# Block attention feeding a gated long convolution on one core: contiguous key loads for the first twelve heads, another order of the first head's work, and copies moved between engines

## The chip, the cores and the metric

The kernel runs on one core of one Trainium2 chip. The metric is device time in microseconds of one launch, lower is better. A core has five engines with an instruction queue each, which run in the order in which the kernel issues: TensorE (PE, with its weight loads shown as PEld), VectorE (DVE), ScalarE (ACT), GpSimd (POOL) and SyncE (SP), which here only issues DMAs. Instructions wait for one another through semaphores.

## The reference, cut to what matters

Inputs `q`, `k`, `v` have the shape (4, 8, 768, 64): 4 batches of 8 heads, so 32 heads of 768 positions, 64 wide.

```
k_rep = k.reshape(B, H, 12, 64, D).mean(axis=3)            # one mean key per block of 64
gate_scores = einsum('bhsd,bhnd->bhsn', q, k_rep)          # later blocks are ruled out
top_idx = argsort(gate_scores)[..., -3:]                   # 3 blocks for each query, and its own
scores = q @ k^T / 8, masked to those blocks and causally
attn = softmax(scores);  x = attn @ v                      # x: (4, 768, 512), heads side by side

proj = x @ w_proj;  x1, x2, x3 = its three parts of 512
x2_conv = irfft(rfft(x2) * rfft(filter_fft))               # along the 768 positions
out = (x1 * x2_conv * x3) @ w_out
```

## The kernel before

**Slots.** The program is a loop over slots, three for each head (`n`, `s`), written out by hand: `scores` of the slot, then `normalise` and the outputs' transposes of earlier heads, stores, `diagonals`, the preparation of coming heads (`prepare`, or `prepare_first` for heads 0 and 1), the set-up pieces entered by `at(n, s, ...)`, the convolution units of the batch before, and last `product` of the slot before. No scheduler moves anything: each engine's order is the order of these calls. Ahead of the loop stands a start written out call by call.

**One head.** A head's queries and keys lie in one fp16 tile, `qk16s[n % 3]` (128 partitions x [2, 6, 128]): t = 0 holds the query, and beside it the query's rounding rest (`query_rest` on VectorE, `low_query` on POOL); t = 1 holds the key (`cast_key`, on POOL) and 12 columns that mark its block (`key_mask`, on POOL, from `eblk`, written once for each of the three tiles). The tile has to be turned, so that the 64 + 12 columns become partitions, into `turned[n]` (`qkT`). For heads 0 to 11 (`PE_HEADS = 12`) TensorE does it (`turn_pe`, six transposes each for t = 0 and 1, into a PSUM bank of `ps_one`), and VectorE or ScalarE copies the result out. From head 12 on SP issues a DMA transpose (`turn_query`).

**The gate.** Key sums of a block (`krp`, fp32 products of keys with `eblk`) are formed on TensorE for heads 0 to 11 (`key_sums_mm`, `key_sums_copy`, `key_sums_turn`, `key_sums_split`, which leaves `kr`), and from head 12 on come from accumulating DMAs on POOL's queue (`add_blocks`, `k_blk`) and sums on VectorE. `gate` multiplies queries by them and finds the third highest on VectorE, with `cbias` ruling out later blocks and `ownm` keeping the own one; the result `gm16` is 0 or -1. `turn_mask` transposes it on TensorE, for two heads at a time from head 2 on, and copies it into rows 64 to 75 of the query part of `qkT`. There it meets the 12 block columns of the keys, so that `scores` gets the mask with the same product.

**Scores and products.** `scores` makes 2 to 4 products in a PSUM tile `sps`, ScalarE takes the exponential (`ex`, 1024, 896 or 768 wide by slot), POOL clears what lies above the diagonal, and `product` multiplies by the values.

**Loads.** Each head's `q`, `k` and `v` come by SP in 192 KB, with position `128 c + p` in chunk c of partition p:

```
k_r = k.rearrange("b h (c p) d -> b h p c d", p=P)
nc.sync.dma_start(keys[g][:, i], k_r[divmod(n, H)])
```

A partition thus gets six rows of 256 bytes from six places. `eblk`[p, c, n] says whether position `128 c + p` is in block n. Weights come by POOL's queue, cast to fp16 (`weights`); `wo` is first read by the output unit (`op`) of batch 0, at head 17.

**Warm products.** `warm(times)` issues 128x512 products on zeros into a PSUM tile that nobody reads (`unread`). At the start five stand ahead of the first key sums, two behind head 0's turns, two ahead of head 0's mask.

**The convolution** of a batch runs in 24 slots behind its eight heads: `x2` (X2), its transform (F1, products `f1a`, `f1b` with VectorE's `t` and POOL's `PQ`), `x13a` and `x13b` (X13, `x1sb` on ScalarE, `gx` on VectorE), the inverse (F2, `f2a`, `f2b`, `yes`, `yy`, `yT`) and the output (O, `op`, `osb`). The sines of the transform are made in the start (`phase_mm`, `phase_round`, `phase_turns`, `sines`). All of them share the four `ps_one` banks with the masks' transposes and the turns.

Of the kernel before, what the change touches and what calls it, by code (L numbers as in the profile page):

```python
# [12 lines left out]
ALU = mybir.AluOpType  # L13
# [4 lines left out]
def kernel(  # L18
# [70 lines left out]

    q_r = q.rearrange("b h (c p) d -> b h p c d", p=P)  # L90
    k_r = k.rearrange("b h (c p) d -> b h p c d", p=P)
    v_r = v.rearrange("b h (c p) d -> b h p c d", p=P)
    NH = B * H

# [18 lines left out]
    def load_key(n):  # L113
        g, i = group_of[n]
        if i == 0:
            keys[g] = kpool.tile([P, KG, SC, D], FP32, name="k_nat", tag="k_nat")
        nc.sync.dma_start(keys[g][:, i], k_r[divmod(n, H)])

    def load_query(n):
        queries[n] = hpool.tile([P, SC, D], FP32, name="q_nat", tag="q_nat")  # L120
# [6 lines left out]
    for n in range(3):  # L127
# [16 lines left out]


    eblk = const.tile([P, SC, NBLK], FP32)
    nc.gpsimd.memset(eblk, 0.0)
    nc.gpsimd.affine_select(
        out=eblk[0:64], in_=eblk[0:64], compare_op=ALU.not_equal,
        fill=1.0, base=0, pattern=[[-2, SC], [1, NBLK]], channel_multiplier=0)  # L150
    nc.gpsimd.affine_select(
        out=eblk[64:128], in_=eblk[64:128], compare_op=ALU.not_equal,
        fill=1.0, base=-1, pattern=[[-2, SC], [1, NBLK]], channel_multiplier=0)

# [11 lines left out]
    def key_mask(i):  # L168
        nc.gpsimd.tensor_scalar(qk16s[i][:, 1, :, D:D + NBLK], in0=eblk, scalar1=MASK, scalar2=0.0,
                                op0=ALU.mult, op1=ALU.add)  # L170

    id_f32 = const.tile([H * NBLK, H * NBLK], FP32)
    nc.gpsimd.memset(id_f32, 0.0)
# [10 lines left out]
    def small_constants(half):  # L184
        rows_ = slice(64 * half, 64 * half + 64)
        if half == 0:
            nc.gpsimd.memset(cbias, 0.0)
        nc.gpsimd.affine_select(
            out=cbias[rows_], in_=cbias[rows_], compare_op=ALU.is_ge,
            fill=-CBIG, base=half, pattern=[[2, SC], [0, 2], [-1, NBLK]], channel_multiplier=0)  # L190
        if half == 1:
            for h in range(2):
                nc.gpsimd.tensor_scalar(ownm[:, :, h, :], in0=eblk, scalar1=1.0, scalar2=-1.0,
                                        op0=ALU.mult, op1=ALU.add)

    FC = const.tile([P, HC, F], fp)
    FS = const.tile([P, HC, F], fp)
# [190 lines left out]
                                    qk16s[n % NB].rearrange("p t c s -> p (t c s)"))  # L388


    def turn_pe(n, t, copy):

        if n not in turned:
            turned[n] = augp.tile([P, 2, SC, P], fp, name="qkT", tag="qkT")
        rows_ = D + NBLK if t else P
        tp = ps_one.tile([P, S], fp, name="tp", tag="one", padded_shape=[P, 2 * 512])
        for c in range(SC):
            nc.tensor.transpose(tp[0:rows_, P * c:P * (c + 1)], qk16s[n % NB][:, t, c, 0:rows_],
                                id_f16)
        copy(turned[n][0:rows_, t], tp[0:rows_, :].rearrange("n (c s) -> n c s", c=SC))  # L400

    def cast_value(n):
        vals[n] = v16s[n % NB]
# [330 lines left out]
    for i in range(2):  # L734
        half = slice(2 * i, 2 * i + 2)
        at(3 + i, 1, weights, wp, moe_w_proj, slice(Dm, 2 * Dm), half)
        at(5 + i, 0, weights, wp, moe_w_proj, slice(2 * P * i, 2 * P * (i + 1)), slice(0, DC))
        at(5 + i, 2, weights, wp, moe_w_proj, slice(2 * Dm + 2 * P * i, 2 * Dm + 2 * P * (i + 1)),
           slice(0, DC))
        at(10 + i, 2, weights, wo, moe_w_out, slice(0, Dm), half)  # L740


    nc.vector.memset(lsc, 1.0)
# [20 lines left out]
        fill=1.0, base=0, pattern=[[-1, P]], channel_multiplier=1)  # L764
    for i in range(HC):
        phase_mm(i)
    warm(5)
    for i in range(HC):
        phase_round(i)
        phase_turns(i)  # L770
# [12 lines left out]
    small_constants(1)  # L783
    cast_query(1, nc.scalar.copy)
    sines(0)
    turn_pe(0, 1, nc.scalar.copy)
    key_sums_copy(0)
    key_sums_turn(0)
    turn_pe(0, 0, nc.vector.tensor_copy)
    warm(2)  # L790
    sines(1)
    key_sums_split(0)
    query_rest(1)
    sines(2)
    turn_angles()
    nc.scalar.activation(tw, twf, AF.Sin, bias=0.0, scale=math.pi / S)

    nc.scalar.preload_act_table_set("exp_and_others")
    key_mask(1)
    cast_key(1)  # L800
    low_query(1)
    gate([0])
    key_sums_mm(1, range(SC))
    warm(2)
    turn_mask([0], [nc.scalar.copy])
    key_sums_copy(1)
    key_sums_turn(1)
    turn_pe(1, 1, nc.vector.tensor_copy)
    key_sums_split(1)
    nc.gpsimd.memset(v16s[0][:, :, D:DV], 1.0)  # L810
    cast_value(0)
# [5 lines left out]
        low_query(m)  # L817

    def turn_both(m):
        turn_pe(m, 1, nc.vector.tensor_copy)  # L820
        turn_pe(m, 0, nc.scalar.copy)

    def prepare(n, s):

        for j, group in enumerate(by_block):
            for fn, place in zip((fold_blocks, sum_blocks, None, split_blocks), group[4]):
                if (n, s) == place and fn:
                    fn(j)
        if s == 0:
            for m in key_loads.get(n, [n + 6]):  # L830
                if m < NH:
                    load_key(m)
            for m in [11, 12] if n == 6 else [n + 5] if n < 6 else [n + 6]:
                if m < NH:
                    load_query(m)
            if n + 2 < NH:
                load_value(n + 2)
        if n < 2:
            prepare_first(n, s)
        elif s == 0:  # L840
            if n % 2 == 1 and n + 1 < 10:
                turn_mask([n + 1, n + 2], [nc.scalar.copy] * 2)
            if n + 2 in group_at:
                key_sums_turn(group_at[n + 2])
                key_sums_split(group_at[n + 2])
            if n == 2:
                turn_both(5)
            if n + 4 < PE_HEADS:
                ready_query(n + 4)
        elif s == 1:  # L850
            if n in (6, 8, 10):
                spectrum(n // 2 - 3)
            if PE_HEADS <= n + 4 < NH:
                turn_query(n + 4)
            if PE_HEADS <= n + 5 < NH:
                cast_key(n + 5)
            if n % 2 == 0 and n < NH - 2:
                gate([n + 2, n + 3])
            elif 10 <= n + 1 < NH - 1:
                turn_mask([n + 1, n + 2], [nc.scalar.copy, nc.vector.tensor_copy])  # L860
        else:
            if n + 4 < PE_HEADS:
                turn_both(n + 4)
            if n + 1 < NH:
                cast_value(n + 1)
            for j, group in enumerate(by_block):
                if n in group[3]:
                    add_blocks(j, group[3].index(n))

        if n > 0 and n + 3 in group_at:  # L870
            key_sums_mm(group_at[n + 3], (2 * s, 2 * s + 1))
            if s == 2:
                key_sums_copy(group_at[n + 3])

    def prepare_first(n, s):
        if (n, s) == (0, 0):
            turn_pe(1, 0, nc.vector.tensor_copy)
            gate([1])
            key_mask(2)
            ready_query(2)  # L880
# [25 lines left out]
    for slot in range(max(units) + 1):  # L906
# [26 lines left out]
        for b, fn, *args in units.get(slot, []):  # L933
# [2 lines left out]
            act = fn(stages[b], *args)  # L936
            if act is not None:
                later.append(act)
        if s == 2:
            if PE_HEADS <= n + 5 < NH:  # L940
                cast_query(n + 5, nc.scalar.copy)
            for j, group in enumerate(by_block):
                if (n, s) == group[4][2]:
                    turn_blocks(j)
# [38 lines left out]
```

## Time and profile before

| | |
|---|---|
| Median of 3 runs | 264.23 us (261.85, 264.23, 265.45) |
| Profiled execution, own time | 260.9 us |
| Its span | 259.2 us |
| Mean granted TensorE clock | 0.999 |
| Busy: PE / DVE / ACT / POOL | 230.9 / 198.7 / 181.7 / 169.6 us |
| First scores on TensorE | 13.11 us |
| DMA, mean over the span | 158 GB/s, 115,232 packets, of them 107,328 under 512 bytes |

The profile is one execution. "Busy" is the sum of the durations of an engine's instructions; an idle stretch is put down to what ended it (its releaser, after the arrow). A group's row gives line, engine, operation, what is written and read, shapes, count, busy us, mean ns of one, and idle time ahead of it. A timeline's row gives start, duration, and the like, with the idle time ahead in brackets. The profile writes the names without buffer numbers: `qk` is `qk16s`, `gm` is `gm16s`, `unread` the warm products.

### The profile page before, as it was taken

The page shows a single profiled execution, that of the slowest core. Times are in us where ns is not written, and L with a number is a line of the kernel's source. Part 1 is how long each engine was busy: PE and PEld are TensorE (multiplying, and loading weights), DVE is VectorE, ACT ScalarE, POOL GpSimd, SP SyncE. Part 2 cuts the span into 40 slices and gives each one's busy share as a digit, 9 for nine tenths or more (in the row PEclk, how much of TensorE's full clock was granted, in tenths as well). Part 3 has the DMA queues.
Part 4 walks back from the last instruction along what each step waited for, and adds up shares of the span by engine and source line. Part 5 has one row for each costly group of instructions (what it writes and reads, how often), then busy time and mean ns, then how long its engine had stood idle before and what let it go on. Part 6 is the DMA issues. An engine that isn't in the chain of part 4 may idle for free.

```text
span 259.2 us, 6281 instructions
## 1 busy us (share of the span) xinstructions
PE 230.9 (89%) x2214; PEld 141.5 (55%) x2214; DVE 198.7 (77%) x591; ACT 181.7 (70%) x284; POOL 169.6 (65%) x324
## 2 busy tenths in 40 slices
PE   6688897979898898789999989889999999999994
PEld 3466565556545555546565656555656665454541
DVE  6788789795899698897887978968879635697820
ACT  4567886888868676777787779687867796412463
POOL 7546666876636799986758987776476676137330
PEclk9999999999999999999999999999999999999999
DMA  8999949999896999999999999987382020100056
GB/s 165 218 166 246 245 101 214 212 182 181 129 237 137 217 167 211 200 181 176 194 161 265 173 235 153 259 183 156 61 217 75 4 81 3 56 25 3 0 206 242
DMA packets 115232, 41.05 MB, mean 158 GB/s; under 512 B 107328, under 2 KB 110400, under 8 KB 115200
## 3 DMA queue, kind: packets, MB, share of 16 engines
q1 hardware_dynamic: 110880, 34.61, 65.6%
q0 software_dynamic: 4320, 6.03, 14.0%
q8 instruction: 17, 0.28, 0.5%
q14 instruction: 15, 0.12, 0.1%
HBM read 28.57 MB, written 6.29 MB: 135 GB/s over the span
## 4 chain that ended last, share of the span: by engine, by line
PE 48%; DVE 18%; ACT 14%; POOL 7%; issue 6%; DMA 5%; ACTq 0%; DVEq 0%; POOLq 0%
PE sps L467 8%; PE op L621 6%; ACT ex L470 6%; DMA k_blk<-in_k_dram 5%; PE o L493 4%; PE x13b L586 4%; PE x2b L547 4%; PE x2a L547 3%; ACT qkT L443 3%; DVE t L568 3%; DVE t L571 2%; POOL ex L478 2%; DVE t L567 2%; PE f2b L602 2%; PE krp L279 2%
## 5 line engine op out<-in xcount | busy, mean ns | idle before, releaser
L470 ACT ACTIVATE ex<-sps 128x1024 f16<-128x1024 f32 (+2 forms) x96 | 87.5, 918 | 40.2 <-PE sps L467 33.7
L478 POOL TENSOR_SCALAR_AFFINE_SELECT ex<-ex 128x128 f16<-128x128 f16 (+1 forms) x128 | 48.2, 397 | 48.3 <-ACT ex L470 47.5
L467 PE MATMUL sps<-qkT 76*128 76x384 f16 (+2 forms) x288 | 52.3, 289 | 0.7 <-ACT qkT L443 0.5
L493 PEld LDWEIGHTS <-ex 128*128 128x128 f16 x672 | 32.3, 98 | 22.7 <-issue 5.5
L493 PE MATMUL o<-v,ex 128*128 128x65 f16 x672 | 37.0, 193 | 5.6 <-POOL ex L478 3.0
L586 PEld LDWEIGHTS <-wp 128*128 128x128 f16 x256 | 24.5, 97 | 18.5 <-issue 4.8
L586 PE MATMUL x13b<-xT,wp 128*128 128x384 f16 x108 | 21.9, 325 | 2.8 <-DVE t L571 1.3
L467 PEld LDWEIGHTS <-qkT 76*128 76x128 f16 x288 | 20.5, 97 | 5.3 <-issue 1.1
L621 PE MATMUL op<-wo,yT 128*128 128x512 f16 x96 | 23.0, 378 | 0.0
L614 POOL TENSOR_TENSOR yT<-gx,yy 128x384 f16<-128x384 f32 x16 | 17.4, 1085 | 8.2 <-DVE yy L608 8.2
L586 PE MATMUL x13a<-xT,wp 128*128 128x384 f16 x108 | 22.0, 325 | 0.0
L575 POOL TENSOR_TENSOR PQ<-t,t 128x512 f16<-128x512 f32 x12 | 15.2, 1270 | 8.1 <-DVE t L568 7.5
L382 POOL TENSOR_SCALAR qk<-rem 128x320 f16<-128x320 f32 x32 | 14.6, 457 | 7.3 <-DVE rem L378 5.1
L509 DVE TENSOR_TENSOR xn<-o,rz 128x384 f16<-128x384 f32 x32 | 17.8, 557 | 1.1
L378 DVE TENSOR_TENSOR rem<-q_nat,qk 128x320 f32<-128x320 f32 x32 | 17.5, 546 | 1.3 <-ACT qk L371 0.3
L591 DVE TENSOR_TENSOR gx<-x1sb,x13b 128x384 f32<-128x384 f16 x27 | 14.9, 552 | 4.5 <-ACT x1sb L590 2.5
L624 ACT COPY osb<-op 128x512 f32<-128x512 f32 x24 | 14.0, 584 | 5.7 <-PE op L621 5.0
L360 POOL CAST qk<-k_nat 128x384 f16<-128x384 f32 x31 | 16.8, 541 | 0.0
L404 POOL CAST v<-v_nat 128x384 f16<-128x384 f32 x32 | 16.2, 505 | 0.7 <-DMA v_nat<-in_v_dram 0.6
L576 POOL TENSOR_TENSOR PQ<-t,t 128x512 f16<-128x512 f32 x12 | 15.2, 1266 | 0.0
L443 ACT COPY qkT<-gmp 12x640 f16<-12x640 f16 x21 | 14.3, 680 | 0.9 <-PE gmp L441 0.4
L547 PEld LDWEIGHTS <-xT 128*128 128x128 f16 x96 | 9.3, 97 | 10.3 <-issue 0.7
(152 smaller groups left out, 477.4 us busy)
## 6 DMA issues: line engine op xcount, KB each, us to landing
q_nat<-in_q_dram SPq DMA_DIRECT2D x32, 192.0 KB, 3.7
k_nat<-in_k_dram SPq DMA_DIRECT2D x32, 192.0 KB, 3.9
v_nat<-in_v_dram SPq DMA_DIRECT2D x32, 192.0 KB, 4.1
out_dram<-osb SPq DMA_DIRECT2D x24, 256.0 KB, 2.1
k_blk<-in_k_dram POOLq DMA_DIRECT2D x10, 384.0 KB, 6.1
rows<-in_moe_filter_fft_dram SPq DMA_DIRECT2D x2, 768.0 KB, 5.9
wp<-in_moe_w_proj_dram POOLq DMA_DIRECT2D x6, 256.0 KB, 6.7
wo<-in_moe_w_out_dram POOLq DMA_DIRECT2D x2, 256.0 KB, 6.3
```

Source lines behind the costliest of these rows:

```text
L360: copy(qk16s[n % NB][:, 1, :, 0:D], keys[g][:, i])
L378: nc.vector.tensor_sub(rems[n], q_nat[:, 1:SC], qk16[:, 0, 1:SC, 0:D])
L443: copies[h](turned[n][D:D + NBLK, 0, 1:SC], gmp[64 * h:64 * h + NBLK, P:S].rearrange("n (c s) -> n c s", c=SC - 1))
L467: nc.tensor.matmul(sps[:, col:col + qe - qs], lhsT=turned[n][0:76, 1, kc, :], rhs=qT[0:76, qs:qe], start=True, stop=True, skip_group_check ...
L470: nc.scalar.activation(ex[:, lo:hi], sps[:, lo:hi], AF.Exp, bias=0.0, scale=scale)
L478: nc.gpsimd.affine_select(out=sub, in_=sub, compare_op=ALU.is_ge, fill=0.0, base=0, pattern=[[0, cnt], [1, P]], channel_multiplier=-1)
L493: nc.tensor.matmul(outs[n][:, qc * DE:(qc + 1) * DE], lhsT=ex[:, col + P * j:col + P * (j + 1)], rhs=vals[n][:, kc, 0:DE], start=(gi == 0 ...
L509: nc.vector.tensor_tensor(out=xns[n // 2][:, :, D * (n % 2):D * (n % 2 + 1)], in0=o[:, :, 0:D], in1=rz.to_broadcast([P, SC, D]), op=ALU.mult)
L547: nc.tensor.matmul(pp, lhsT=xT[:, dc, base + P * i:base + P * (i + 1)], rhs=wp[:, dc, Dm:2 * Dm], start=(dc == 0), stop=(dc == DC - 1))
L586: nc.tensor.matmul(dst, lhsT=wp[:, dc2, base:base + P], rhs=xT[:, dc2, hs:hs + HALF], start=(dc2 == 0), stop=(dc2 == DC - 1))
L614: nc.gpsimd.tensor_mul(yT[:, dc, S - 1:HALF - 1:-1], st["g"][:, dc, 1, :], yy[:, 1, :])
L621: nc.tensor.matmul(op, lhsT=yT[:, cc, P * scn:P * (scn + 1)], rhs=wo[:, cc, :], start=(cc == 0), stop=(cc == DC - 1))
```

## The change

- Keys of heads 0 to 11 are loaded by another view, `k_runs`: position `6 p + c` in chunk c of partition p, so a partition gets 1,536 bytes in a run. Queries, values and the later heads' keys stay.
- The order is put right when the turned keys are copied from PSUM: column `128 c + p` goes to position `6 p + c`. This copy is now ScalarE's (`take_keys`) for all twelve heads, and the queries' copy is VectorE's (`take_queries`). Before, VectorE copied the keys and ScalarE the queries, other than for heads 0 and 1.
- `eblk` marks blocks in the new order. `ownm`, which needs the old one, is made by itself (`own_blocks`), and the block columns of the three `qk16s` tiles are written anew for heads 12, 13 and 14 (`key_mask_by_chunks`).
- The start has another order: three warm products ahead of the first key sums instead of five, and three instead of two ahead of head 0's mask; `key_sums_split(0)` ahead of the queries' copy; `gate([0])` ahead of head 1's key mask and cast; head 1's keys are turned ahead of head 0's mask.
- `turn_mask` copies both heads' masks on ScalarE for heads below 24 (before, from head 9 on, one on ScalarE and one on VectorE).
- `cast_query(n + 5)` comes a slot earlier when n is even.
- The two loads of `wo` move from heads 10 and 11 to heads 14 and 15.

```diff
+    k_runs = k.rearrange("b h (p c) d -> b h p c d", p=P)
...
-        nc.sync.dma_start(keys[g][:, i], k_r[divmod(n, H)])
+        nc.sync.dma_start(keys[g][:, i], (k_runs if n < PE_HEADS else k_r)[divmod(n, H)])
...
-    nc.gpsimd.memset(eblk, 0.0)
+    nc.gpsimd.memset(eblk, 1.0)
     nc.gpsimd.affine_select(
-        out=eblk[0:64], in_=eblk[0:64], compare_op=ALU.not_equal,
-        fill=1.0, base=0, pattern=[[-2, SC], [1, NBLK]], channel_multiplier=0)
+        out=eblk, in_=eblk, compare_op=ALU.is_ge,
+        fill=0.0, base=0, pattern=[[1, SC], [-64, NBLK]], channel_multiplier=SC)
     nc.gpsimd.affine_select(
-        out=eblk[64:128], in_=eblk[64:128], compare_op=ALU.not_equal,
-        fill=1.0, base=-1, pattern=[[-2, SC], [1, NBLK]], channel_multiplier=0)
+        out=eblk, in_=eblk, compare_op=ALU.is_ge,
+        fill=0.0, base=63, pattern=[[-1, SC], [64, NBLK]], channel_multiplier=-SC)
...
+    def key_mask_by_chunks(i):
+        nc.gpsimd.tensor_scalar(qk16s[i][:, 1, :, D:D + NBLK], in0=ownm[:, :, 0, :], scalar1=1.0,
+                                scalar2=MASK, op0=ALU.add, op1=ALU.mult)
...
-        if half == 1:
-            for h in range(2):
-                nc.gpsimd.tensor_scalar(ownm[:, :, h, :], in0=eblk, scalar1=1.0, scalar2=-1.0,
-                                        op0=ALU.mult, op1=ALU.add)
+    def own_blocks(half):
+        rows_ = slice(64 * half, 64 * half + 64)
+        if half == 0:
+            nc.gpsimd.memset(ownm, -1.0)
+        nc.gpsimd.affine_select(
+            out=ownm[rows_], in_=ownm[rows_], compare_op=ALU.not_equal,
+            fill=0.0, base=half, pattern=[[2, SC], [0, 2], [-1, NBLK]], channel_multiplier=0)
...
-    def turn_pe(n, t, copy):
+    def turn_pe(n, t):
...
-        copy(turned[n][0:rows_, t], tp[0:rows_, :].rearrange("n (c s) -> n c s", c=SC))
+        turned_pe[n, t] = tp
+
+    def take_keys(n):
+        tp = turned_pe.pop((n, 1))
+        rows_ = D + NBLK
+        nc.scalar.copy(turned[n][0:rows_, 1].rearrange("n c s -> n (c s)").rearrange(
+                           "n (p c) -> n c p", c=SC),
+                       tp[0:rows_, :].rearrange("n (c p) -> n c p", c=SC))
+
+    def take_queries(n):
+        tp = turned_pe.pop((n, 0))
+        nc.vector.tensor_copy(turned[n][:, 0], tp.rearrange("n (c s) -> n c s", c=SC))
...
-        at(10 + i, 2, weights, wo, moe_w_out, slice(0, Dm), half)
+        at(14 + i, 2, weights, wo, moe_w_out, slice(0, Dm), half)
...
-    warm(5)
+    warm(3)
...
-    turn_pe(0, 1, nc.scalar.copy)
+    turn_pe(0, 1)
+    take_keys(0)
     key_sums_copy(0)
+    sines(1)
     key_sums_turn(0)
-    turn_pe(0, 0, nc.vector.tensor_copy)
+    key_sums_split(0)
+    turn_pe(0, 0)
+    take_queries(0)
     warm(2)
-    sines(1)
-    key_sums_split(0)
-    query_rest(1)
+    own_blocks(0)
+    own_blocks(1)
     sines(2)
     turn_angles()
...
+    gate([0])
+    key_sums_mm(1, range(SC))
+    warm(3)
     key_mask(1)
     cast_key(1)
+    turn_pe(1, 1)
+    query_rest(1)
     low_query(1)
-    gate([0])
-    key_sums_mm(1, range(SC))
-    warm(2)
     turn_mask([0], [nc.scalar.copy])
+    take_keys(1)
     key_sums_copy(1)
     key_sums_turn(1)
-    turn_pe(1, 1, nc.vector.tensor_copy)
     key_sums_split(1)
...
     def turn_both(m):
-        turn_pe(m, 1, nc.vector.tensor_copy)
-        turn_pe(m, 0, nc.scalar.copy)
+        turn_pe(m, 1)
+        take_keys(m)
+        turn_pe(m, 0)
+        take_queries(m)
...
             if PE_HEADS <= n + 5 < NH:
+                if n + 5 < PE_HEADS + NB:
+                    key_mask_by_chunks((n + 5) % NB)
                 cast_key(n + 5)
...
-                turn_mask([n + 1, n + 2], [nc.scalar.copy, nc.vector.tensor_copy])
+                turn_mask([n + 1, n + 2],
+                          [nc.scalar.copy, nc.scalar.copy if n < 24 else nc.vector.tensor_copy])
...
+        if s == 1 + n % 2 and PE_HEADS <= n + 5 < NH:
+            cast_query(n + 5, nc.scalar.copy)
         if s == 2:
-            if PE_HEADS <= n + 5 < NH:
-                cast_query(n + 5, nc.scalar.copy)
```

More of the change, by code (lines that the diff above doesn't have):

```diff
@@ L399, in turn_pe @@
                                 id_f16)
[L400 removed]
+        turned_pe[n, t] = tp
+    turned_pe = {}
+    def take_keys(n):
[7 more added lines that the diff above has]
+        nc.vector.tensor_copy(turned[n][:, 0], tp.rearrange("n (c s) -> n c s", c=SC))
     def cast_value(n):
@@ L876, in prepare_first @@
         if (n, s) == (0, 0):
-            turn_pe(1, 0, nc.vector.tensor_copy)
+            turn_pe(1, 0)
+            take_queries(1)
             gate([1])
```

## The prediction, made before the changed kernel had run

> **What bounds the kernel now.** I read the busy times first, then the stretches, then the waits of the engines, and last the timelines of the two places that the change touches most. Busy times, and three stretches (columns: stretch, then busy us and instructions of PE, PEld, DVE, ACT, POOL; granted clock; DMA share; GB/s):
>
> ```profile
> PE 230.9 (89%) x2214; PEld 141.5 (55%) x2214; DVE 198.7 (77%) x591; ACT 181.7 (70%) x284; POOL 169.6 (65%) x324
> ```
>
> ```profile
> 0.00:10.00 10.00, 6.88 (x50) 3.71 (x51) 6.92 (x25) 4.08 (x6) 7.76 (x29) 1.00 1.03 183
> ...
> 90.00:100.00 10.00, 8.86 (x95) 5.46 (x94) 9.83 (x27) 6.89 (x12) 9.13 (x16) 1.00 1.14 180
> ...
> 250.00:260.00 10.00, 5.43 (x26) 2.24 (x23) 0.00 (x0) 4.10 (x8) 0.00 (x0) 0.94 0.65 237
> ```
>
> TensorE is the busiest engine everywhere, and only its gaps can be won: 259.2 - 230.9 = 28.3 us of idle. Some 5 us of that lie ahead of the first scores and 4 to 5 in the drain of the last stores, so at most 18 to 19 us are left between. Inside, VectorE is nearly full in places (9.83 of 10 at 90 to 100 us), ScalarE seldom.
>
> TensorE's start, from its own timeline (start us, us, what, idle before and its releaser):
>
> ```profile
> 3.01 2.31 PE L757 MATMUL unread<-gm 128*128 128x512 f16 x5
> 5.25 1.25 PE L279 MATMUL krp<-k_nat,eblk 128*12 128x64 f32 x12
> ...
> 7.54 0.59 PE L757 MATMUL unread<-gm 128*128 128x512 f16 x2
> 9.22 0.29 PE L417 MATMUL gps<-kr,qkT 128*128 128x24 f16 x5 [1.09 <-DVE kr L310]
> 9.44 0.84 PE L279 MATMUL krp<-k_nat,eblk 128*12 128x64 f32 x12
> 10.21 0.60 PE L757 MATMUL unread<-gm 128*128 128x512 f16 x2
> 11.89 0.44 PE L441 MATMUL gmp<-id_f,gm 128*12 128x128 f16 x5 [1.08 <-DVE gm L430]
> ```
>
> Nothing of attention runs until the chain key sums, gate, mask has gone through; scores begin at 13.11. ScalarE takes head 0's keys at 4.53, so they have landed, but TensorE is in its five unread products until about 5.3 and starts krp then: 0.8 us late. The gate waits 1.09 us for kr on VectorE, which had taken the query copy (7.74, 0.56 us) and a sine addition (8.21, 0.56 us) first.
>
> Who waited for whom (total us, times, longest):
>
> ```profile
> DVE qkT L443 <- ACT qkT L443: 6.2, 8, 1.0
> ...
> PE f2b L602 <- DVE qkT L443: 2.1, 2, 1.1
> ```
>
> The mask copies: ScalarE takes one head's, VectorE the other's, and VectorE sits idle for it. Twice TensorE waits 1.05 to 1.1 us for that second copy; at 115.92 VectorE came to it late, behind 2.6 us of block sums (L334, L338).
>
> Groups with their shapes (count, busy us, mean ns, idle before):
>
> ```profile
> L443 ACT COPY qkT<-gmp 12x640 f16<-12x640 f16 x21 | 14.3, 680 | 0.9 <-PE gmp L441 0.4
> L443 DVE COPY qkT<-gmp 12x640 f16<-12x640 f16 x11 | 5.4, 489 | 6.3 <-ACT qkT L443 6.2
> ...
> L400 ACT COPY qkT<-tp 128x768 f16<-128x768 f16 x10 | 8.0, 804 | 0.3 <-PE tp L398 0.3
> L400 DVE COPY qkT<-tp 76x768 f16<-76x768 f16 x11 | 6.0, 549 | 3.6 <-PE tp L398 3.6
> ...
> L422 DVE TENSOR_TENSOR g<-gps,ga 128x120 f32<-128x120 f32 x15 | 4.2, 282 | 0.5
> L428 DVE TENSOR_TENSOR get<-g,m 128x120 f32<-128x120 f32 x15 | 7.6, 509 | 0.5
> ```
>
> **1. The new order up to head 0: -1.1 us.** Three unread products at 2.31/5 = 0.46 us each end at 3.01 + 1.39 = 4.4; krp can start with the keys at 4.5 and ends at 5.7 (6.5 before). VectorE's queue: rest of query 0 until 5.58, first sine addition until 6.05, then the two sum copies (0.21 and 0.18) until 6.45, the second sine addition (0.56) until 7.0, the two kr operations (0.22, 0.23) until 7.5, and only then the query copy (0.56) until 8.1. Gate at 8.15 against 9.22. The third sine addition (0.56) now stands ahead of the gate's own operations, which start at about 8.9 against 9.95 and take 1.89 as before (9.95 to 11.84): masks at 10.8. ownm now costs POOL a clearing and two selects over 64x144, priced by cbias (0.22 + 0.86) against 0.46 for the two operations that go: +0.6 us, done at 8.8, two us before the mask needs it. Behind it key 1's cast ends at about 9.8 instead of 9.1; key 1's turn on TensorE then stands at 9.95, behind gate, krp (0.84) and three warm products at 0.3. query_rest(1) goes behind the gate's operations; its reader, query 1's turn, stands behind scores at 12.0. Mask transposes 10.85, mask copy 11.3 to 12.0, scores at 12.05 against 13.11. ScalarE now takes key 1 (0.8) ahead of the first exponential, which starts at 12.8 against 13.74. So -0.9 to -1.1; I take -1.1. Bounds: -2.0 if the first keys, with shorter transfers, also land earlier; +0.5 if three products leave TensorE slow for longer: 12 passes of krp took 1.25 us at 5.25 and 0.84 at 9.44, which is 0.4 for such a piece.
>
> The Trainium skill (TensorE: Matmul & The Clock Gate, Part 1) says that the array runs at half rate until about 4 us of sustained work, give or take half. The trace agrees: work began at 1.97, krp at 5.25 was slow, six transposes at 6.44 took 0.53 like later ones. By that rule the change is safe only if keys land before the third product ends; the bound of +0.5 would otherwise be the term.
>
> **2. Keys in runs: 0, bounds -0.6 and +7.7.** In the first 10 us nothing but these loads moves: 183 GB/s over 16 engines at a share of 1.03 is 11.1 GB/s each, 23 ns for a 256-byte row. The last stretch, with stores of 2 KB rows, gives 237/(16 x 0.65) = 22.8, so 67 ns for a run of 1,536 bytes. A key load falls from 768 x 23/16 = 1.10 us to 128 x 67/16 = 0.54; twelve save 6.8 us of the 16 engines. But SP issues all twelve by 40 us, two heads ahead of use, and in that time the only waits for a load that show are the first keys (2.4 us), a query (0.4) and a value (0.6). So it is worth nothing behind head 0, and up to -0.56 there.
>
> The copy that puts them in order: ScalarE wrote 76x768 once in 0.79 us, and writes 128x768 in 0.804 ten times; VectorE's key copies (0.549) go, and its query copies (0.557) come. One copy each per head as before, and ScalarE's is now the one that is ready first. The new thing is its write with a step of 12 bytes, which no row of before shows. From below: the ScalarE rows of 128x384 read backwards (L519) took 496 ns against 474 forwards (L518), so +0.04 for 768. From above: VectorE's get (L428), with a repeated, stepped operand, took 509 against 282 for the like L422; 1.8 x 0.794 = 1.43, that is +0.64 a copy. ScalarE is the nearer engine, so I take 0.80 and no change. At the upper price: of the twelve copies some seven stand where ScalarE runs on into an exponential without a gap (18.55, 20.06, 28.19, 31.89, 56.99, 61.76 and the new one at 12), 7 x 0.64 = 4.5 us; all twelve 7.7.
>
> The Trainium skill speaks against this edit (SBUF — State Buffer, the note on "cachelines"): accesses that stay in a 16-byte line run at full rate, and each that crosses into a new line pays. With 12-byte steps three of four cross. No row of before shows it; by it the sum would carry the 4.5.
>
> key_mask_by_chunks adds three POOL operations of 0.25 us for heads 12 to 14, ahead of the key's cast and so of the low query and the DMA transpose queued behind. POOL's idle time ahead of the selects (47.5 us in total) covers them; uncovered, 0.75. eblk's selects keep their size per partition: 0.
>
> **3. Both masks on ScalarE, heads 9 to 23: -1.1 us.** Eight VectorE copies of 0.489 and its 6.2 us of waiting go; eight of 0.68 come to ScalarE. At the two block-sum heads (copies at 115.38 and 166.50) ScalarE is through at 114.35 and 165.4, and f2b follows f2a: -1.05 and -1.09. In the other places (102.23, 153.28) VectorE took over the moment ScalarE was done, so the bank is free 0.68 - 0.49 = 0.19 us later than now, and x1sb and the 768-wide exponential come 0.68 later; its reader on TensorE stood about 0.5 off (exponential done at 103.5, select 0.3, product at 104.37). I charge 0.2 at five places, +1.0. Sum -1.1. Bounds: +5.4 (8 x 0.68, if ScalarE leads everywhere) and -5.1 (half of VectorE's 3.9 + 6.2, if its freed time reaches TensorE).
>
> **4. cast_query one slot earlier for even heads: -0.5; weights later: 0.** The cast (0.52) goes ahead of the 768-wide exponential where no mask copy is; the rest, low query and DMA transpose behind it can follow sooner, and one gate waited 1.1 us for a DMA transpose. Half of that, bounds -1.1 and +0.5. The two wo loads (0.9 us of POOL issue each, 6.3 to landing) pass from heads 10 and 11 to 14 and 15 on POOL's queue, out of the block sums' transfers and into those of the DMA transposes; their first reader is at head 17, some 13 us later. Uncovered, half a microsecond either way.
>
> **Sum.** -1.1 + 0 - 1.1 - 0.5 + 0 = -2.7 us. The profiled execution took 260.9 us around a span of 259.2; it would take 258.2 around 256.5. The three runs have a median of 264.23, 3.3 above that execution; taken off the median, 261.5. A measurement of this kernel tells about 2% (5.3 us) from no change.
>
> **Rivals.** *VectorE's release carries (256.9).* If the freed 10.1 us (8 x 0.489 + 6.2) lets half through, and the start gives 1.7: 264.23 - 5.1 - 1.7 - 0.5 = 256.9. For it: VectorE at 9.83 of 10, and TensorE's waits for t, kr, gm and xn. Against it: the waits lie just behind its full stretches, not in them.
> *The stepped write is dear (265.6).* ScalarE's copy at 1.43 us: 261.5 + 4.5 = 266.0, less 0.4 that key copies win by being ready first = 265.6, slower than now; with all twelve on the path 268.8. It overtakes the gains from 2.7/7 = 0.39 us a copy on. For it: ScalarE is busy 38.5 of 48 us from 20 to 68. Against it: no ScalarE row is hurt by its pattern by more than 5%.
> *ScalarE becomes the bound at heads 9 to 23 (268).* All 5.4 us of new copies on the path: 264.23 - 1.1 - 0.5 + 5.4 = 268.0. For it: at 102 and 153 it runs copy, x1sb, exponential without a gap. Against it: its exponentials wait 33.7 us in all for TensorE.
>
> **How the numbers follow.** Forecast 0.43, VectorE's release 0.34, stepped write 0.15, ScalarE's bound 0.08. The forecast's own bounds are -4.7 to +1.0 on the median. The range must reach over the second rival and to the third's middle: 255.5 to 266.5. Faster by over 2%: the second case nearly whole (0.32) and the forecast's edge (0.06). Slower by over 2% (269.5): the stepped write with all twelve on the path and other losses, 0.09, ScalarE's bound, 0.05. Rest 0.48.
>
> **What would show it.** Right: krp starting at 4.4 to 4.6, gate at 8.2, first scores at 12.1; the key copy at 0.8 to 0.85 us; no wait of f2b for a mask copy; VectorE 10 us less busy or waiting, ScalarE 5 to 6 us more busy. Wrong: a key copy over 1.2 us; krp still at 5.3; exponentials of 768 that lead TensorE's waits after 68 us; a TensorE that is idle less than 24 us in all.

## The result, and the profile after

The changed kernel took 278.92 us (median of four runs, 276.79 to 281.52) against 263.72 us for the kernel before beside it: a ratio of 1.0551 (95% interval 1.0431 to 1.0671), slower. The profiled execution took 276.79 us around a span of 275.1. Ratios here leave disturbed runs out, so that one need not be the quotient of two medians.

Busy times of the changed kernel, then ScalarE and the granted TensorE clock in 40 slices of 6.9 us (tenths), and the chain of waits by engine:

```profile
PE 238.8 (87%) x2213; PEld 147.4 (54%) x2213; DVE 194.1 (71%) x582; ACT 207.2 (75%) x293; POOL 170.4 (62%) x328
...
ACT  4999799898998867697778777887786787432463
PEclk9999559799799999999999999999999999999999
...
PE 40%; ACT 27%; DVE 18%; issue 8%; POOL 6%; ACTq 0%; POOLq 0%; DVEq 0%
```

ScalarE is 25.5 us busier than before (181.7). TensorE is busier by 7.9 us with one instruction fewer, so it has no more work but does it more slowly; and its idle time is 275.1 - 238.8 = 36.3 us, 8.0 more. The clock line points to what the 7.9 are: in the first third the clock falls, in two slices to a digit of 5, half speed. The chain of waits now runs through ScalarE for 27% of the span.

The groups of instructions name the operation (count, busy us, mean ns of one, idle before):

```profile
L419 ACT COPY qkT<-tp 76x768 f16<-76x768 f16 x12 | 32.7, 2729 | 0.9 <-PE tp L409 0.8
L425 DVE COPY qkT<-tp 128x768 f16<-128x768 f16 x12 | 6.7, 556 | 10.5 <-PE tp L409 10.4
```

The key copy with the stepped write costs 2.73 us; the prediction took 0.80, and 1.43 at most. Twelve times the 1.93 above that is 23.2 us, nearly the whole growth of ScalarE.

ScalarE's timeline (start us, us, what):

```profile
6.90 2.72 ACT L419 COPY qkT<-tp 76x768 f16<-76x768 f16 x1 [0.32 <-PE tp L409]
...
12.91 2.72 ACT L419 COPY qkT<-tp 76x768 f16<-76x768 f16 x1
15.25 1.23 ACT L495 ACTIVATE ex<-sps 128x1024 f16<-128x1024 f32 x1
...
22.21 2.73 ACT L419 COPY qkT<-tp 76x768 f16<-76x768 f16 x1
24.55 2.03 ACT L495 ACTIVATE ex<-sps 128x1024 f16<-128x1024 f32 x2
26.47 2.72 ACT L419 COPY qkT<-tp 76x768 f16<-76x768 f16 x1
30.57 0.81 ACT L495 ACTIVATE ex<-sps 128x768 f16<-128x768 f32 x1 [1.39 <-PE sps L492]
```

A copy stands ahead of the first exponential, which starts at 15.25 instead of 13.74, and two stand around the pair at 24.55. TensorE's timeline at the start and behind the copy of 26.47:

```profile
4.63 1.44 PE L290 MATMUL krp<-k_nat,eblk 128*12 128x64 f32 x12 [0.16 <-POOL dft_ka L230]
...
9.67 0.27 PE L442 MATMUL gps<-kr,qkT 128*128 128x24 f16 x5 [1.51 <-ACT qkT L419]
...
29.24 0.60 PE L518 MATMUL o<-v,ex 128*128 128x65 f16 x8 [2.88 <-ACT qkT L419]
```

And the stretches there (stretch, busy us and instructions of PE, PEld, DVE, ACT, POOL; granted clock; DMA share; GB/s):

```profile
24.00:26.00 2.00, 1.38 (x18) 1.04 (x17) 1.90 (x14) 2.00 (x3) 1.10 (x3) 1.00 0.09 23
26.00:28.00 2.00, 0.36 (x4) 0.17 (x2) 1.83 (x7) 2.00 (x2) 1.41 (x4) 0.99 0.74 124
28.00:30.00 2.00, 0.76 (x10) 0.59 (x10) 0.46 (x1) 1.19 (x1) 0.95 (x3) 0.50 0.87 329
30.00:32.00 2.00, 2.00 (x13) 1.15 (x12) 0.00 (x0) 1.40 (x2) 0.55 (x2) 0.50 0.83 240
...
42.00:44.00 2.00, 1.93 (x23) 1.16 (x24) 0.75 (x2) 1.95 (x4) 1.06 (x3) 1.00 0.51 128
```

One copy may be paid twice here. TensorE waits 2.88 us for it, until 29.24; the clock drops to 0.50 at about 28, when the four microseconds before held 1.38 + 0.36 = 1.74 us of TensorE's work, and stays there until about 41.5. In most of that time TensorE is full (9.94 us of the ten from 30 to 40) at half speed, and ScalarE now waits for it once (1.39 us for scores). Whether this second payment shows in the total is taken up below. The Trainium skill (TensorE: Matmul & The Clock Gate, Part 1) says that the array goes back to half rate after an idle window of some 3.4 us; this stretch differs, for the clock fell some 1.6 us into the wait, and the 3.4 us before were not idle. Some ten microseconds of full work passed before the clock came back.

Where it was lost: the 1024-wide exponentials, which open each head, start 1.5 us later than before at head 0, 3.8 at head 1, 9.0 at head 3, 15.2 at head 8 (78.21 against 63.04), and 14.8 at head 12 (106.02 against 91.27). The loss lies where the twelve copies lie. Behind them 1.1 us more go, up to head 25 (15.9), and then nothing.

### The profile page after: what moved, and what is told of

It is laid out like the page before. It is cut to its first block, busy times and chain, and to the rows that moved or that the text cites. A ratio compares the mean times of both kernels' runs of the same rounds, so it can differ in the third digit from the quotient of the medians.

```text
span 275.1 us, 6268 instructions
## 1 busy us (share of the span) xinstructions
PE 238.8 (87%) x2213; PEld 147.4 (54%) x2213; DVE 194.1 (71%) x582; ACT 207.2 (75%) x293; POOL 170.4 (62%) x328
## 4 chain that ended last, share of the span: by engine, by line
PE 40%; ACT 27%; DVE 18%; issue 8%; POOL 6%; ACTq 0%; POOLq 0%; DVEq 0%
ACT ex L495 10%; ACT qkT L419 8%; PE op L646 7%; PE sps L492 6%; ACT qkT L468 4%; PE x13b L611 3%; PE o L518 3%; PE x2b L572 3%; PE x2a L572 3%; DVE t L596 2%; DVE t L592 2%; DVE gx L616 2%; DVE t L593 2%; POOL ex L503 2%; PE x13a L611 1%
## 5 line engine op out<-in xcount | busy, mean ns | idle before, releaser
L495 ACT ACTIVATE ex<-sps 128x1024 f16<-128x1024 f32 (+2 forms) x96 | 89.1, 936 | 33.7 <-PE sps L492 27.1
L503 POOL TENSOR_SCALAR_AFFINE_SELECT ex<-ex 128x128 f16<-128x128 f16 (+1 forms) x128 | 47.4, 384 | 65.2 <-ACT ex L495 64.6
L492 PE MATMUL sps<-qkT 76*128 76x384 f16 (+2 forms) x288 | 54.7, 299 | 0.0
L518 PEld LDWEIGHTS <-ex 128*128 128x128 f16 x672 | 33.3, 100 | 27.0 <-issue 8.7
L518 PE MATMUL o<-v,ex 128*128 128x65 f16 x672 | 38.2, 197 | 8.7 <-POOL ex L503 3.6
L419 ACT COPY qkT<-tp 76x768 f16<-76x768 f16 x12 | 32.7, 2729 | 0.9 <-PE tp L409 0.8
L468 ACT COPY qkT<-gmp 12x640 f16<-12x640 f16 x29 | 19.7, 680 | 1.2 <-PE gmp L466 0.5
L393 POOL TENSOR_SCALAR qk<-rem 128x320 f16<-128x320 f32 x32 | 14.7, 460 | 9.2 <-DVE rem L389 4.7
L600 POOL TENSOR_TENSOR PQ<-t,t 128x512 f16<-128x512 f32 x12 | 15.3, 1271 | 8.1 <-DVE t L593 7.5
L409 PE MATMUL tp<-id_f,qk 128*76 128x128 f16 (+1 forms) x144 | 13.8, 254 | 3.1 <-ACT qkT L419 1.1
L429 POOL CAST v<-v_nat 128x384 f16<-128x384 f32 x32 | 16.2, 507 | 0.1
L371 POOL CAST qk<-k_nat 128x384 f16<-128x384 f32 x31 | 15.8, 509 | 0.0
```

Of the source, the lines that this page charges most:

```text
L419: nc.scalar.copy(turned[n][0:rows_, 1].rearrange("n c s -> n (c s)").rearrange("n (p c) -> n c p", c=SC), tp[0:rows_, :].rearrange("n (c p ...
L468: copies[h](turned[n][D:D + NBLK, 0, 1:SC], gmp[64 * h:64 * h + NBLK, P:S].rearrange("n (c s) -> n c s", c=SC - 1))
L492: nc.tensor.matmul(sps[:, col:col + qe - qs], lhsT=turned[n][0:76, 1, kc, :], rhs=qT[0:76, qs:qe], start=True, stop=True, skip_group_check ...
L495: nc.scalar.activation(ex[:, lo:hi], sps[:, lo:hi], AF.Exp, bias=0.0, scale=scale)
L503: nc.gpsimd.affine_select(out=sub, in_=sub, compare_op=ALU.is_ge, fill=0.0, base=0, pattern=[[0, cnt], [1, P]], channel_multiplier=-1)
L518: nc.tensor.matmul(outs[n][:, qc * DE:(qc + 1) * DE], lhsT=ex[:, col + P * j:col + P * (j + 1)], rhs=vals[n][:, kc, 0:DE], start=(gi == 0 ...
```

## The experiments

### The copy by itself

The theory: it is the write's step that costs, in itself. Rivals: the read, or something around the copy in the kernel. This kernel computes nothing of the reference; it makes each form of a copy of 76x768 three times, alone.

```
nc.scalar.copy(h[0:R, 0:S], src[0:R, 0:S])                       # L44: f16, in a run
nc.scalar.copy(h[0:R, 0:S*k].rearrange("n (s k) -> n s k", k=k)[:, :, 0], src[0:R, 0:S])  # L45 to L49: k = 2, 3, 4, 6, 8
# L50 to L54: the same into f32, k = 1, 2, 3, 4, 6.  L55: the kernel's own form.
# L56: its loops exchanged (writes in a run, reads PSUM with a step).  L60 to L70: VectorE.
```

> This kernel computes nothing of the reference: it only copies 768 values a partition (76 partitions), three times in each form, so that one copy can be timed by its form. First theory, the step of the write is what costs: ScalarE writes 2-byte values in a run in 0.8 us, at a step of 12 bytes in about 2.7 us, and with the loops exchanged (write in a run, read with a step) in 0.8 to 0.9 again; the price should rise somewhere between steps of 4 and 16 bytes. If 16-byte lines are the unit, a step of 4 bytes costs little, 12 and 16 bytes cost the same. Second theory, any stepped pattern costs ScalarE, read or write: exchanged loops also take 2.7 us. Third theory, only the three-dimensional pattern costs (six runs of 128): the plain step of 6 in one dimension is cheap, 0.8 us. VectorE's forms tell whether the cost is ScalarE's own (VectorE stays at 0.55) or the memory's (VectorE rises too, to 1 us or more).

Its groups (PSUM source; mean ns of one is the second number behind the bar):

```profile
L49 ACT COPY h<-src 76x768 f16<-76x768 f16 x3 | 10.6, 3546 | 0.1
...
L55 ACT COPY h<-src 76x768 f16<-76x768 f16 x3 | 8.2, 2721 | 0.1
L48 ACT COPY h<-src 76x768 f16<-76x768 f16 x3 | 8.1, 2706 | 0.1
L69 DVE COPY g<-sr 76x768 f16<-76x768 f16 x3 | 8.1, 2704 | 0.1
...
L47 ACT COPY h<-src 76x768 f16<-76x768 f16 x3 | 5.6, 1870 | 0.1
...
L46 ACT COPY h<-src 76x768 f16<-76x768 f16 x3 | 4.3, 1434 | 0.1
...
L45 ACT COPY h<-src 76x768 f16<-76x768 f16 x3 | 3.0, 1008 | 0.1
L70 DVE COPY g<-sr 76x768 f16<-76x768 f16 x3 | 2.9, 954 | 0.1
...
L44 ACT COPY h<-src 76x768 f16<-76x768 f16 x3 | 2.4, 794 | 0.1
L56 ACT COPY h<-src 76x768 f16<-76x768 f16 x3 | 2.4, 794 | 0.1
```

The price is the write's: steps of 2, 4, 6, 8, 12 and 16 bytes take 794, 1008, 1434, 1870, 2706 and 3546 ns, a straight line from 4 bytes on, some 210 ns for each further byte of step. VectorE pays the same (2,704). The three-dimensional pattern adds nothing: the kernel's own form takes 2,721, the plain step of 12 bytes 2,706. Exchanging the two loops makes the price vanish on ScalarE: 794. An f32 result is cheaper at the same step (12 bytes: 1,178 ns; 24 bytes: 1,498), so it is not the distance alone.

### Two ways to undo the stepped write alone

With keys by chunks and a plain copy (all else as changed), and with keys in runs and the loops exchanged:

```
 e1  take_keys: nc.scalar.copy(turned[n][0:rows_, 1], tp[...].rearrange("n (c s) -> n c s", c=SC))
     and eblk, k_r as before
 e2 -    "n (p c) -> n c p", c=SC), tp[0:rows_, :].rearrange("n (c p) -> n c p", c=SC))
    +    "n (p c) -> n p c", c=SC), tp[0:rows_, :].rearrange("n (c p) -> n p c", c=SC))
```

> The changed kernel with keys loaded by chunks as before, the block marks in that order, and ScalarE's key copy in a run; the new start, both masks on ScalarE, the earlier casts and the later weights all stay. First theory (the stepped copy is the whole loss, 12 x 1.93 us on ScalarE): the copy is back at 0.8 us and the time at 260 to 264. Second theory (the loss is ScalarE's load in general, with the masks, or the order): the time stays above 268.

> The changed kernel with the two loops of the key copy exchanged: it writes in a run and reads PSUM with a step of 256 bytes; the same values go to the same places. If the write's step is the cost, the copy takes 0.8 to 0.9 us and the time is 259 to 263, the changed kernel as it was meant. If a stepped read costs as much, the copy stays near 2.7 us and the time near 279.

By chunks: 262.32 us, ratio 0.9993 (0.9965 to 1.0021). Loops exchanged: 262.10 us, 0.9995 (0.996 to 1.003). The copy and the clock with the loops exchanged:

```profile
PEclk9999999999999999999999999999999999999999
...
L419 ACT COPY qkT<-tp 76x768 f16<-76x768 f16 x12 | 9.5, 792 | 0.6 <-PE tp L409 0.5
```

One line of the kernel, the order of two loops in one copy, carries the whole loss. The two kernels of this pair differ in the key loads too, and agree within 0.1%, with intervals of 0.3%: no worth of the loads in runs shows, although the share of the DMA engines that SP's queue (q1) takes falls from 64.7% to 62.5%.

### The stepped copy on VectorE

If only ScalarE were short of time, VectorE, which then gives its query copies to ScalarE, should bear the price better.

```
-nc.scalar.copy(turned[n][0:rows_, 1]...)     +nc.vector.tensor_copy(turned[n][0:rows_, 1]...)
-nc.vector.tensor_copy(turned[n][:, 0], ...)  +nc.scalar.copy(turned[n][:, 0], ...)
```

> The changed kernel with VectorE doing the stepped key copy, and ScalarE the queries' copy. If the cost is ScalarE's own, VectorE takes 0.55 us and the time is 260 to 264. If the memory charges each write into a new line, VectorE takes 1.2 to 2.7 us as well, and the time is 268 to 280.

288.75 us, ratio 1.1019 (1.0946 to 1.1093); the copy took 2,716 ns there. Worse than either theory: the price is not ScalarE's own, and VectorE's queue now stands behind the copy (GpSimd's wait for the queries' rest `rem` on VectorE is 16.2 us, against 4.7 as changed).

### How much is ScalarE's time, how much the step itself

From the kernel with the loops exchanged, the cheap copy is made two and three times, and, as the match of the stepped copy's time, three times with one of 128 columns ahead:

```
 e7  take_keys: the copy in a run, twice        e11: three times
 e13 +nc.scalar.copy(turned[n][0:rows_, 1, 0], tp[0:rows_, 0:P])      # and the copy in a run, three times
```

> The changed kernel with the loops of the key copy exchanged (0.79 us a copy) and each key copy made twice, so that ScalarE has 12 x 0.79 = 9.5 us more work without any stepped write. If what the stepped write costs is just ScalarE's time, the loss is in proportion to the changed kernel's (16.8 us lost for 12 x 1.94 = 23.2 us more): 6.9 us, a time of 269. By my count of seven copies on the path it is 7 x 0.79 = 5.5, 267.6. If ScalarE's slack takes the first part whole, and only the long copy breaks the order, it is under 3 us: below 265.

> The changed kernel with exchanged loops and each key copy made three times: 12 x 1.59 = 19.0 us more on ScalarE, no stepped write. With 9.5 us more the time rose by only 2.3, with the stepped write's 23.2 by 16.8. If ScalarE has some 7 us of slack over heads 0 to 11 and the rest comes out one for one, 19.0 - 7.0 = 12 us: 274 (272 to 276). If the stepped write hurts by more than its time on ScalarE (the clock, the memory), this one stays below 270.

> The changed kernel with the stepped key copy replaced by three copies with exchanged loops and a fourth piece of 128 columns, which together hold ScalarE about as long as one stepped copy (some 2.55 us from start to start of the next). Three copies alone gave 271.2 us at a mean granted clock of 0.978, the stepped copy 278.9 at 0.95. If the stepped write hurts by ScalarE's time alone, through a steep end of the curve (gaps on TensorE grow, its clock falls, the gaps' work takes longer), this kernel stands at 275 to 280 with a clock of 0.95 to 0.965. If it hurts in another way as well, this one stays at 271 to 274 with a clock of 0.97 or more.

| Kernel | ScalarE busy, us | Ratio to before (95%) | TensorE busy, idle, us | Mean granted clock |
|---|---|---|---|---|
| loops exchanged | 186.0 | 0.9995 (0.996-1.003) | 231.5, 28.5 | 1.000 |
| copy twice | 194.7 | 1.0091 (1.0052-1.0131) | 231.6, 29.6 | 0.998 |
| three times | 203.9 | 1.0358 (1.0308-1.0408) | 235.9, 34.0 | 0.981 |
| matched | 207.0 | 1.0458 (1.0411-1.0506) | 239.0, 33.7 | 0.962 |
| as changed | 207.2 | 1.0551 (1.0431-1.0671) | 238.8, 36.3 | 0.960 |

(Busy, idle and clock are those of the profiled execution; idle is the span less busy.) The first 8.7 us on ScalarE cost 2.5 us (0.0096 x 262), the next 9.2 cost 7.0, and with these the clock falls. Three copies (271.19 us) and the match (274.2) came out between what their two theories had said. The stretch of the matched kernel, where ScalarE is full and TensorE slow:

```profile
30.00:40.00 10.00, 8.29 (x90) 6.40 (x87) 6.93 (x34) 9.76 (x16) 4.27 (x11) 0.68 0.49 132
```

With ScalarE busy as long as in the changed kernel and no stepped write, 0.0458 of the 0.0551 are there. The two intervals overlap, so ScalarE's time is enough for most of the loss, perhaps all. The pieces hold ScalarE no shorter than the stepped copy does: from their start to the end of the exponential behind it is 3.67 us (12.40 to 16.07), with the stepped copy 3.57 (12.91 to 16.48). Whether one long copy hurts more than four short ones stays open.

The time doesn't follow the clock among the four runs of the matched kernel: 274.42 us at a mean clock of 0.962, 273.94 at 0.987. So the clock falls along with TensorE's gaps, but here no cost of its own shows.

### TensorE kept busy

Two kernels meant to split the loss between the clock and the waits. One adds two warm products to each slot of the first nine heads; the other makes the score products of heads 0 to 9 twice, some 13 us of TensorE work, and both keep the stepped write.

```
 e8  +        if n < 9:
     +            warm(2)
 e15 -for kc, qs, qe, col in pieces:   +for kc, qs, qe, col in pieces * (2 if n < 10 else 1):
```

> The changed kernel with two unread products more in each slot of heads 0 to 8 (54 of 0.22 to 0.3 us in place of idle time), so that TensorE has fewer long gaps. In the changed kernel the granted clock fell to 0.5 at 30 to 40 us and the mean to 0.96. If the fallen clock carries part of the loss, the clock stays at 1.0 and the time drops by 2 to 5 us, to 274 to 277. If the clock only falls where TensorE waits for ScalarE anyway, the time is unchanged or up to 5 us longer, 279 to 284.

> The changed kernel with every product of the scores made twice for heads 0 to 9, into the same place: 0.43 us more work for TensorE in a slot, 13 us in all, with no more banks or waits. In the changed kernel TensorE is idle some 14 us between 13 and 83 us. If the fallen clock carries 5 us or more of the loss, the clock rises to 0.98 or more and the time falls below 277. If the work just adds to the chain, 280 to 286 at whatever clock.

The kernel with the warm products took 292.4 us (1.1194, 1.111 to 1.1279), beyond either theory, and says nothing of the clock, since these products brought waits of their own: they read one of the two `gm16s` tiles, so they stand behind the gate that writes it, and others stand behind key copies. Who waited for whom in that kernel:

```profile
PE unread L782 <- DVE gm L455: 7.6, 3, 4.2
PE unread L782 <- ACT qkT L419: 4.5, 4, 1.5
```

The doubled scores took 279.11 us (1.0627, 1.0563 to 1.0692): by the ratios 0.0076, some 2 us, above the changed kernel, with intervals that overlap, for 13 us more work on the busiest engine. That is neither of the two theories. At a granted clock of 0.98 to 0.994 its runs took 277.76, 278.06 and 280.17, the changed kernel's at 0.939 to 0.960 took 276.79, 277.89 and 279.95. Two readings fit: the work filled gaps that ScalarE leaves anyway, or it was paid by the clock that it kept up. Within each kernel the longest of these runs is the one at the lowest clock, which speaks for the second; the matched kernel speaks against it. The runs don't tell them apart, and what the fallen clock costs stays open.

### The new start, and the masks, each alone

The kernel before with the new order up to head 0 (keys by chunks, masks, casts and weights as before), and the kernel before with both mask copies on ScalarE for heads below 24:

```
 e5   warm(3), key copies, sums, sines, gate and own_blocks in the new order
 e6  -turn_mask([n + 1, n + 2], [nc.scalar.copy, nc.vector.tensor_copy])
     +turn_mask([n + 1, n + 2], [nc.scalar.copy, nc.scalar.copy if n < 24 else nc.vector.tensor_copy])
```

> The kernel before with the new order of the start alone (warm products, gate, head 1's turn, ownm by itself); keys by chunks, the turned keys of heads 2 to 11 copied by VectorE and the queries by ScalarE, masks, casts and weights as before. With the loops of the key copy exchanged, the first exponential came at 12.70 us against 13.74, but at head 8 at 62.97 against 63.04. First theory: the other moves (copies exchanged between ScalarE and VectorE, masks) take the start's 1.0 us back; then it stands at the end here: the first exponential of head 8 at 62.0 or earlier, the time 261.4 against 262.4. Second theory: the later heads absorb any earlier start, because their pace is set by waits further on; then head 8 is within 0.3 us of 63.04 here too, and the time is the same.

> The kernel before with both masks copied by ScalarE for heads below 24, and nothing else. My prediction held that this wins 1.1 us; the heads' starts with exchanged loops point the other way (equal to before at head 16, 0.8 us later at head 25). First theory, it loses 0.5 to 1 us between heads 12 and 25: time 262.9 to 263.4 against 262.4. Second theory, it wins 1.1: 261.3, and the loss belongs to the earlier casts or the later weights.

The start alone: 260.97 us, 0.9956 (0.992 to 0.9991), so -1.1 us. The masks alone: 263.75 us, 1.0018 (0.9975 to 1.006), nothing. The start's lead over before, by the first exponential, was 1.2 us at head 0 and still 0.9 at head 8 (62.17 against 63.04). VectorE's wait for x1sb in the kernel before, then its waits with the masks on ScalarE:

```profile
DVE gx L591 <- ACT x1sb L590: 3.1, 5, 0.9
...
DVE gx L591 <- ACT x1sb L590: 12.6, 8, 2.9
...
DVE qkT L443 <- ACT qkT L443: 2.2, 3, 1.0
```

(VectorE's wait, what it waited for, total us, times, longest.) The wait for the mask copy fell from 6.2 to 2.2 us, and that for x1sb, behind the two mask copies on ScalarE, rose from 3.1 to 12.6. VectorE's wait is later, not gone. From head 12's first exponential to head 31's this kernel took 120.5 us, against 120.4 before.

### The start with keys in runs, and the block sums spaced

With the loops exchanged and masks, casts and weights as before (e9); the same with the first four loads of block sums at heads 2, 4, 6, 7 (e10); that spacing in the kernel before alone (e12); and with the new start alone (e14). GpSimd waits 2 to 5 us for these loads (3.2 before), and I thought that they ate part of the earlier start.

```
-        (12, 8, 1, [4, 5, 6, 7], [(9, 0), (9, 1), (9, 2), (10, 0)]),
+        (12, 8, 1, [2, 4, 6, 7], [(9, 0), (9, 1), (9, 2), (10, 0)]),
```

> The changed kernel with the loops of the key copy exchanged, and masks, casts and weights as before: so the new start, keys in runs, and ScalarE copying keys while VectorE copies queries. The start alone took the time to 260.97 (ratio 0.9956). If keys in runs bring something beyond the start, 259 to 260.5 (ratio 0.988 to 0.993). If the lighter transfers are hidden anyway, as I predicted, the same as the start alone: 260.5 to 261.5. If exchanging the copies costs, 262.

> The same with the four transfers of the first block sums issued at heads 2, 4, 6 and 7 instead of 4, 5, 6 and 7. POOL waits 3.2 us for these in the kernel before, 3.6 with exchanged loops, 4.8 where only the start is new, and what is issued behind it (the selects) is late by that. First theory, this chain of transfers gives the start's gain back by head 9: POOL's wait falls to 1.5 us or less, the first exponential of head 9 stands at 68 or earlier, the time is 258.5 to 260. Second theory, the wait is slack of POOL's: time as without the move, within 0.5 us.

> The kernel before with the first block sums' transfers at heads 2, 4, 6 and 7, and nothing else. If this chain of transfers paces heads 5 to 9, it gains by itself 0.5 to 2 us (260.3 to 261.7 against 262.2) and POOL's wait of 3.2 us falls to 1.5 or less. If it is slack, no change.

> The new order of the start alone, with the first block sums' transfers at heads 2, 4, 6 and 7. The start alone stood at 0.9956 of the kernel before; with exchanged loops the spacing took 0.9993 to 0.9955. If the spacing keeps the start's gain, 0.991 to 0.994 (259.9 to 260.6); if the two overlap, 0.9955 again.

| Kernel | Median, us | Ratio to before (95%) |
|---|---|---|
| start, keys in runs | 261.5 | 0.9993 (0.9962-1.0025) |
| the same, spaced | 260.27 | 0.9955 (0.9925-0.9985) |
| before, spaced | 262.18 | 0.9996 (0.9961-1.0032) |
| start alone, spaced | 260.44 | 0.9945 (0.9912-0.9978) |

Spacing takes GpSimd's wait away (2.8 to 0.8 us with keys in runs, 3.2 to none before) and by itself wins nothing. With the start it gives the best kernel of the study, 0.55% under before, though not told apart from the start alone (0.9956). In e10 head 9's first exponential stands at 69.22 us, not at 68 as the theory had it. Start and keys in runs together, without the spacing (0.9993), don't show the gain of the start alone (0.9956); the intervals overlap, so this is no sign of a loss either.

## Why the prediction was wrong

**The step that failed is the price of the stepped write**, in part 2: "ScalarE is the nearer engine, so I take 0.80", with 1.43 as the upper price. Measured: 2.73. The bounds weren't bounds of this operation. The lower came from reading backwards (L519), the upper from a VectorE read with a repeated operand (L428); both are reads, and the copy by itself shows that on ScalarE reads with a step are cheap (794 ns from PSUM, 1,208 at 12 bytes from SBUF) where writes are dear. No row of before wrote single elements at a distance, so "from above" was a guess by likeness. The upper row wasn't a price of its pattern either (shortest, median and longest in ns):

```profile
L428 DVE TENSOR_TENSOR get<-g,m x17: 282/497/1115, 10.9 to 198.8; 128x120 f32<-128x120 f32 x15, 128x60 f32<-128x60 f32 x2
```

With one and the same pattern it takes 282 ns at its shortest, as long as L422, and 1,115 at 108.10 us, while GpSimd's yT (L614, 1.00 us from 108.07) runs beside it. The 1.8 is a mean over such places.

**The rival had the mechanism, with half the price.** "The stepped write is dear" had seven of twelve copies on the path. At 1.93 us each its own sum is 261.5 + 7 x 1.93 = 275.0, and with all twelve 284.7; 278.9 lies between. Measured from the kernel with the loops exchanged, the stepped write costs 0.0556 of 264, 14.7 us, or 7.6 copies of 1.93; whether these are seven copies and something of the clock, or more copies, the runs don't separate. Most of what is left of the miss is the 2.7 us of gains in the sum: with the copy at its forecast price (e2) the kernel wins 0.1 us (0.9995). The prediction's own sign of error, a key copy over 1.2 us, showed at once.

**The Trainium skill (SBUF — State Buffer, the note on "cachelines") pointed the right way**: it speaks against the edit, and was put at 4.5 us of the rival. Its free range is not what was measured: steps that stay inside a 16-byte line are not free (4 bytes 1,008 ns, 8 bytes 1,870 against 794), and nothing jumps at 16.

**The new start: right in its sum.** With the stepped write gone and the rest as changed (e2), krp started at 4.84 (forecast 4.5), the gate at 8.69 (8.15), scores at 12.03 (12.05), the first exponential at 12.70 (12.8); alone it won 1.1 us, as forecast. That the scores came to the hundredth is luck: the gate came 0.5 us late, and its operations on VectorE started 0.4 us behind it instead of 0.75 and took 1.57 us (9.12 to 10.69) instead of 1.89. TensorE was slow for longer, as the upper bound had it: krp took 1.44 us against 1.25, and the two turns behind it 0.86 and 0.82 against 0.53 and 0.51. In e2 the lead is 1.0 us at head 0 and 0.1 at head 8 (62.97 against 63.04). With the stepped write the same gate stands at 9.67, behind the key copy.

**Keys in runs, the loads: right, 0,** as far as the runs can tell. The pair of undoings agrees within 0.1%.

**Both masks on ScalarE: wrong by its whole 1.1.** f2b's wait for the second mask copy (2.1 us) did go, as forecast. But the copy that VectorE no longer makes is one that x1sb now stands behind, and VectorE waits there. The charge for that, +1.0 at five places, was probably too small by as much as the gain; no run separates the two. "VectorE's release" (256.9) fails on the same lines. ScalarE as the bound at heads 9 to 23 (268) fails too: the masks alone stand at 1.0018, not 5.4 us above before.

**Casts earlier, weights later: -0.5 not seen.** No run tested them alone; with masks, casts and weights (0.9995) and without (0.9993) the kernel is the same.

## What to carry to other kernels

Where a copy has to change an order, let it read with the step and write in a run: the same copy of 76x768 took 0.79 us that way and 2.72 the other. Price an access pattern that no row shows by a row of the same side, a write by a write; if there is none, the upper bound is open, and the range should say so. An engine with slack takes the first microseconds of extra work cheaply, but not the next: here 8.7 us on ScalarE cost 2.5, the 9.2 after them 7.0.

## What the runs showed of the hardware

- ScalarE and VectorE pay for the step of a 2-byte write alike: 2,706 and 2,699 ns for 768 elements at 12 bytes. VectorE reading PSUM with a step takes 954 ns where in a run it takes 553; ScalarE takes 794 for both.
- The granted TensorE clock fell to 0.50 for some 13 us in the middle of a kernel in which TensorE is busy 87% of the span, after four microseconds with 1.74 us of work.
- The granted clock also goes with the small spread between runs of one kernel: of the kernel before beside e5, six runs at a clock of 1.0 took 260.21 to 261.08 us, five at 0.985 to 0.987 took 263.06 to 264.03. In e5's profile the clock stood at 0.50 from 66.4 to 69.8 us, and the kernel went from 0.9 us ahead of before at head 8 to 1.1 behind at head 10. So half a per cent can't be told from one run.
